# Chunk 1 of a two-product kernel in Strassen groups that accumulate on copies, with a new order of work

## The chip, the cores and the metric

The kernel runs on one core of a Trainium2 chip. The metric is device time in microseconds (us) of one execution; the median over several executions is compared. A core has a matrix engine (PE, with its weight loads PEld), three engines for element-wise work (DVE, which is VectorE; ACT, which is ScalarE; POOL, which is GpSimd) and SP (SyncE), which here only starts transfers. Matmuls write PSUM, a buffer of eight banks of 512 float32 per partition; SBUF is the other on-chip memory. Each engine takes its instructions in order and waits on semaphores for the others.

## The reference

Attention with linear cost comes first, then two matrix products with a SiLU between them. Shapes: q, k, v are (8 batches, 8 heads, 576 positions, 64), w_in is (512, 2048), w_out is (2048, 512), all float32.

```python
q_s = softmax(q over the 64 features)
k_s = softmax(k over the 576 positions)
kv  = k_s^T @ v                    # 64 x 64 for each batch and head
x   = q_s @ kv                     # regrouped as 4608 tokens x 512
h   = x @ w_in                     # 4608 x 2048
out = silu(h) @ w_out              # 4608 x 512
```

## The kernel before

**Stages.** Tokens are worked on in chunks of 512 (`TCH`), numbered 0 to 8. Chunk 0 is done as batch 0's whole 576 tokens, so chunk 1 holds only 448 new ones. For each batch `b` the kernel loads halves of q, k and v (`lq`, `lk`, `lv`, two halves each, 576 KB a half), takes exponentials on ACT (`eq`, `ek`), sums and normalises q (`z`, `n`), casts v (`vc`), transposes q (`tr` with copies `tc` for batches 0 and 1, a DMA transpose `tq` after them), multiplies k by v on PE (`kv`), normalises the result (`kc`), and multiplies q by it (`xt1` or `X`), which is copied out of PSUM as x (`x`, the suffix `a` or `v` says whether ACT or DVE does it).

**The first product** (x by w_in). Chunk 0 does 16 blocks `w0` to `w15` with 288-column matmuls, each followed by a tanh on ACT (`h`) and a multiply on DVE (`v`), which make the SiLU. Chunks 2 to 8 use a Strassen scheme (Winograd's form) with seven products in place of eight. The 2048 columns of w_in are split in two groups, g = 1 and g = 0; a group does products 1, 2, 6, 5, 7, 4, 3 of 8 matmuls each (`g{chunk}.{group}.{product}`), on operands that DVE has prepared (`WS` from w_in, `xs` from x). Products 1, 6, 7 and 4 accumulate in banks 0 and 1. After 1, 6 and 7 the running sum is copied to SBUF (`s`, line 400). Products 2, 5 and 3 go to another bank pair, and DVE adds each result to one of the copies (`a`, line 403). SiLU on ACT (`u`, line 409) reads three sums from SBUF and one from PSUM. Chunk 1 is half and half: group 1 so, with 224 columns, and group 0's eight blocks as plain products, `m0` to `m7`, four matmuls of 448 columns (line 335), with a SiLU each (`mu`, line 345).

**The second product** (by w_out). Chunk 0 does it plainly, `p0` to `p15`: block `p{i}` needs rows 128i to 128i+127 of w_out, and all four output tiles stand in banks 2 to 5 until `po` copies them out. Chunks 1 to 8 use Strassen products `b{chunk}.{product}.{half}` in banks 4 and 5 (line 503); `S` and `T` (line 487) are their operands, `sa`, `sb`, `sc`, `wa`, `wb`, `wc`, `wl` take the sums out, and `o` stores them. `e` are the products of the last chunk.

**Order.** One string, `ORDER`, lists every operation after a written-out start; the program calls them in that order, and each engine's queue is this list cut down to its own instructions. Nothing is reordered later. POOL starts all transfers of w_in (`load_w1`, line 564), w_out (`load_w2`: W2a, W2b1, W2b2, W2c1, W2c2, W2d, line 570) and of batches 1 and 2; SP starts the rest and the stores.

**Around the change.** W2b1 brings the rows for p4 and p5, W2b2 those for p6 and p7, W2c1 for p8 and p9, W2c2 for p10 and p11, W2d for p12 to p15. `kv1` needs v of batch 1, whose casts are `vc1.0` (whole, ACT), `vc1.1a` and `vc1.1b` (a half each on ACT and DVE). Buffers of loaded halves are two deep. `gcopy` and the `po` copies run on ACT and DVE between chunk 0's second product and chunk 1's first. The SiLU function and the exponential need different ACT tables; a change from one to the other is an `ACT_TABLE_LOAD`.

Of the kernel before, what the change touches and what calls it, by code (L numbers as in the profile page):

```python
# [8 lines left out]
FP32 = mybir.dt.float32  # L9
BF16 = mybir.dt.bfloat16  # L10
FP16 = mybir.dt.float16
ACT = mybir.ActivationFunctionType
# [6 lines left out]
    lk1.0 w1 lk1.1 w2 h1 w0 h2 v1 w3 h0 W2b1 w5 v0 v2 h3 w4 WS0.1 h5 w6 v3 h4 W2b2 v4 w7 v5 w8 h7 h6 v7 w9  # L19
    lv1.0 h8 v6 w11 v8 h9 lv1.1 w10 eq1.0.0 v9 h11 WS0.2 w12 eq1.1.0 v11 h10 w13 WS1.1 eq1.0.1 v10 h12 w15  # L20
    qp1a h13 v12 w14 eq1.1.1 v13 qp1b WS1.2 W2c1 p0 h14 z1.0 ek1.0 p1 z1.1.0 n1.0 z1.1.1 p2 h15 ek1.1 v15 p3
    WS1.4 W2c2 tr1.0 v14 lq2.0 p4 tc1.0a tc1.0b lq2.1 n1.1 p5 W2d p6 lk2.0 T1 vc1.0 lk2.1 p7 tr1.1 lv2.0
    vc1.1a vc1.1b gcopy WS1.3 kv1 lv2.1 tc1.1b p8 tc1.1a kc1 WS0.3 xt1.0 xt1.1 x1.0a x1.1v p9 x1.2a x1.3v
    g1.1.1 xs1.1 xs1.2 xs1.4 g1.1.2 s1.1.0a WS0.4 p10 xs1.3 eq2.0 a1.1.0 p11 eq2.1 z2.0 g1.1.6 g1.1.5
    s1.1.1a z2.1 n2.0 p12 ek2.0 g1.1.7 p13 s1.1.2v n2.1 ek2.1 p14 a1.1.2 g1.1.4 p15 tq2 u1.1.4 g1.1.3 po2v
    vc2.1 po1a m0 po3v po0a a1.1.1 u1.1.0 vc2.0 m1 lk3.0 mu0 m2 T2 lq3.0 mu1 lq3.1 m3 u1.1.2 lk3.1 T3 m4
    lv3.0 u1.1.1 lv3.1 m5 T4 mu2 os0 mu4 kv2 mu5 m6 mu3 kc2 X2.0 mu6 X2.1 x2.0v m7 x2.1a x2.3a x2.2v g2.1.1
    mu7 xs2.1 xs2.2 g2.1.2 s2.1.0v b1.1.0 ek3.0 S1.1 g2.1.6 eq3.1 lk4.0 S1.2 b1.2.0 os1 s2.1.1a b1.1.1 xs2.3
# [36 lines left out]
    qa10a e5.1 sc8 wcE0 e3.0 wcE1 qc01g wxE0 qc11a e3.1 wbE0 qc00a wxE1 qb00g qb01s e4.0 wbE1 qc10s qb10g
    e4.1 qb11s wlE0a ql01a ql00s wlE1a ql11a ql10s
# [4 lines left out]
def kernel(  # L71
# [206 lines left out]
    def xt_mm(b, cc, col, n, bank, dst):  # L278
        for r in range(2):
            for s in range(2):  # L280
                h = slice(s * 64, (s + 1) * 64)
                nc.tensor.matmul(  # L282
                    out=PS[r * 64:(r + 1) * 64, bank + s, dst:dst + n],
                    lhsT=kvn[b % 3][h, cc, r, :],
                    rhs=st[b]["qT"][h, col // P:(col + n) // P, cc, r * 64:(r + 1) * 64],
                )
# [44 lines left out]

    def mm1_mm(t, fb, bank, cs):
        o0 = pieces(t)[0][3]
        for c in cs:
            nc.tensor.matmul(  # L335
                out=PS[:, bank, o0:TCH],
                lhsT=W1[:, c, fb * 128:(fb + 1) * 128],
                rhs=XTS[t % 2][:, c, o0:TCH],
                start=(c == 0),
                stop=(c == NC - 1),  # L340
            )

    def mm1_out(t, fb, bank):
        o0 = pieces(t)[0][3]
        nc.scalar.activation(
            out=GTS[t % 2][:, fb, o0:TCH], in_=PS[:, bank, o0:TCH], func=ACT.Silu, scale=1.0 / XS
        )

    H = [None] * 3
# [38 lines left out]
    def four(t, i):  # L388
        return H[i].rearrange("p (f n) -> p f n", f=4)[:, :, 0:width(t)]

    def other(t, g):
        return 6 if t == 1 or g else 2

    def group_bank(t, g):
        bank = 0 if g is None else other(t, g)
        return PS[:, bank:bank + 2, :].rearrange("p b (f n) -> p (b f) n", f=2)[:, :, 0:width(t)]

    def group_snap(t, i, eng):
        H[i] = mp.tile([128, 2 * TCH], FP32, name=f"h{i}", bufs=1)
        copy(eng, four(t, i), group_bank(t, None))  # L400

    def group_add(t, g, i):
        nc.vector.tensor_tensor(  # L403
            out=four(t, i), in0=group_bank(t, g), in1=four(t, i), op=ALU.add
        )

    def group_silu(t, i, f, n):
        x = group_bank(t, None) if i is None else four(t, i)
        nc.scalar.activation(out=group_out(t, f, n), in_=x, func=ACT.Silu, scale=1.0 / XS)  # L409
# [429 lines left out]
```

## Time and profile before

| what | value |
|---|---|
| median of 3 executions | 257.08 us (256.99 to 257.14) |
| the profiled execution, whole | 258.61 us |
| the profiled execution, span of its instructions | 256.6 us |
| PE busy | 249.1 us, 97% |
| DVE, ACT, POOL busy | 206.2, 190.9, 65.8 us |
| groups' adds (line 403) | 45, mean 1206 ns |
| copies to SBUF on ACT (line 142, 1024 columns) | 29, mean 1010 ns |
| copies to SBUF on DVE (line 144, 1024 columns) | 13, mean 1222 ns |
| SiLU from SBUF / from PSUM (line 409, 1024 columns) | 1056 / 1020 ns |
| ACT table loads | 16, 1283 ns each |

A row of the timeline gives start (us from the span's start), length, engine, source line, operation, output and input with their shapes, and the count when several were merged; in square brackets is the engine's idle time before it and what ended that. Ends of matmuls are modelled, so the distance between starts is the safer measure. A row of the windows gives a stretch, its length, busy time and count of PE, PEld, DVE, ACT and POOL, the granted clock, the DMA engines' busy share (a 1 is all sixteen) and GB/s.

### The profile page before, as it was taken

What the parts mean: (1) busy time and instruction counts of PE and PEld (TensorE: products, weight loads), DVE (VectorE), ACT (ScalarE), POOL (GpSimd) and SP (SyncE); (2) the same over time, 40 slices, a digit from 0 to 9 for tenths busy, and PEclk for the clock granted to TensorE, in tenths of its full rate; (3) what the DMA queues carried; (4) which work ended last, traced back from release to release, by engine and by line L of the source; (5) the groups of instructions that cost most, each with busy time, mean ns of one, the idle gap of its engine ahead of it and who ended that gap; (6) DMA issues with size and microseconds to landing.
All of it is one profiled execution on the core that took longest, in us unless ns stands there. A gap on an engine that the chain in (4) does not pass through costs nothing.

```text
span 256.6 us, 6459 instructions
## 1 busy us (share of the span) xinstructions
PE 249.1 (97%) x2732; PEld 204.2 (80%) x2732; DVE 206.2 (80%) x276; ACT 190.9 (74%) x225; POOL 65.8 (26%) x62
## 2 busy tenths in 40 slices
PE   8799999999999999999999999999999999999994
PEld 3457746656888888888888888888888888888883
DVE  2958999888999898998987986896579836886752
ACT  5766876699999999999879988737587665664411
POOL 1753593650450622350073030006000000000022
PEclk9999999999999999999999999999999999999999
DMA  7999999979959957996874960021807000600365
GB/s 248 348 181 297 302 301 283 351 140 393 378 128 213 403 187 137 361 335 168 276 266 68 224 236 3 3 52 32 163 14 153 13 0 4 148 18 0 66 141 123
DMA packets 36044, 45.89 MB, mean 179 GB/s; under 512 B 16288, under 2 KB 21088, under 8 KB 36016
## 3 DMA queue, kind: packets, MB, share of 16 engines
q1 hardware_dynamic: 29456, 33.56, 45.5%
q0 software_dynamic: 6160, 11.60, 17.8%
q10 hardware_dynamic: 400, 0.33, 0.6%
q8 instruction: 21, 0.34, 0.5%
q14 instruction: 7, 0.06, 0.1%
HBM read 36.70 MB, written 9.44 MB: 180 GB/s over the span
## 4 chain that ended last, share of the span: by engine, by line
PE 76%; DMA 11%; issue 5%; POOL 3%; ACT 2%; DVE 1%; ACTq 0%; POOLq 0%
PE PS L503 37%; PE PS L425 33%; DMA qt<-in_q_dram 5%; DMA kt<-in_k_dram 5%; PE PS L335 3%; PE PS L248 2%; PE PS L282 2%; POOL W L564 1%; DMA out_dram<-ow 1%; POOL qt L152 1%; DVE GT L323 1%; ACT L409 0%; POOL W L570 0%; ACT sg L320 0%; ACT GT L409 0%
## 5 line engine op out<-in xcount | busy, mean ns | idle before, releaser
L403 DVE TENSOR_TENSOR h<-PS,h 128x1024 f32<-128x1024 f32 (+1 forms) x45 | 54.2, 1206 | 9.3 <-PE PS L425 7.8
L503 PEld LDWEIGHTS <-GT 128*128 128x128 f16 x512 | 50.1, 98 | 5.9
L425 PEld LDWEIGHTS <-WS 128*128 128x128 f16 x480 | 46.7, 98 | 6.5 <-issue 0.6
L409 ACT ACTIVATE GT<-h 128x1024 f16<-128x1024 f32 (+1 forms) x45 | 46.8, 1051 | 0.9 <-DVE h L403 0.7
L503 PE MATMUL PS<-W,GT 128*128 128x256 f16 x384 | 47.3, 273 | 0.0
L425 PE MATMUL PS<-XS,WS 128*128 128x256 f16 (+1 forms) x360 | 45.0, 272 | 0.0
L142 ACT COPY h<-PS 128x1024 f32<-128x1024 f32 (+1 forms) x31 | 31.1, 1003 | 16.9 <-PE PS L425 15.7
L503 PEld LDWEIGHTS <-S 128*128 128x128 f16 x384 | 37.1, 98 | 4.6
L425 PEld LDWEIGHTS <-W 128*128 128x128 f16 x360 | 35.2, 98 | 4.4
L216 POOL TENSOR_TENSOR eq<-eq,rzq 128x1152 bf16<-128x1152 bf16 x13 | 27.3, 2115 | 37.6 <-DVE rzq L211 36.3
L503 PE MATMUL PS<-T,S 128*128 128x256 f16 x256 | 32.2, 273 | 0.0
L144 POOL CAST vaug<-vt 128x1152 bf16<-128x1152 f32 x12 | 15.8, 1328 | 61.5 <-DMA vt<-in_v_dram 61.4
L425 PE MATMUL PS<-XT,W 128*128 128x256 f16 (+1 forms) x240 | 29.7, 272 | 0.0
L144 DVE COPY h<-PS 128x1024 f32<-128x1024 f32 (+1 forms) x14 | 17.0, 1212 | 9.2 <-PE PS L425 4.4
L207 DVE TENSOR_REDUCE zq<-eq 128x18 f32<-128x1152 bf16 x14 | 18.8, 1342 | 4.1 <-ACT eq L163 4.0
L163 ACT ACTIVATE eq<-qt 128x1152 bf16<-128x1152 f32 (+1 forms) x18 | 18.9, 1055 | 3.1 <-DMA qt<-in_q_dram 2.8
L168 ACT ACTIVATE ek<-kt 128x1152 bf16<-128x1152 f32 x16 | 18.6, 1163 | 3.0 <-DMA kt<-in_k_dram 2.9
L791 POOL DMA_DIRECT2D out_dram<-ow x5 | 2.7, 545 | 70.0 <-DVE ow L773 70.0
L409 ACT ACTIVATE GT<-PS 128x1024 f16<-128x1024 f32 (+1 forms) x15 | 15.2, 1013 | 6.1 <-PE PS L425 6.1
L503 PE MATMUL PS<-T,GT 128*128 128x256 f16 x128 | 16.3, 272 | 0.0
L307 PE MATMUL PS<-XT,W 128*128 128x288 f16 x128 | 16.0, 286 | 0.2 <-DMA W<-in_moe_w_in_dram 0.2
L503 PE MATMUL PS<-W,S 128*128 128x256 f16 x128 | 16.1, 273 | 0.0
(85 smaller groups left out, 332.4 us busy)
## 6 DMA issues: line engine op xcount, KB each, us to landing
out_dram<-ow SPq DMA_DIRECT2D x64, 128.0 KB, 3.0
qt<-in_q_dram SPq DMA_DIRECT2D x11, 576.0 KB, 5.9
kt<-in_k_dram SPq DMA_DIRECT2D x11, 576.0 KB, 7.5
vt<-in_v_dram SPq DMA_DIRECT2D x11, 576.0 KB, 6.6
qt<-in_q_dram POOLq DMA_DIRECT2D x4, 576.0 KB, 11.4
kt<-in_k_dram POOLq DMA_DIRECT2D x4, 576.0 KB, 13.9
vt<-in_v_dram POOLq DMA_DIRECT2D x4, 576.0 KB, 12.6
W<-in_moe_w_in_dram POOLq DMA_DIRECT2D x3, 512.0 KB, 10.6
```

Of the source, the lines that this page charges most:

```text
L142: eng.copy(out=o, in_=i)
L144: eng.tensor_copy(o, i)
L163: nc.scalar.activation(out=half(st[b]["eq"], cc)[:, :, g0:g1], in_=jgd(b, "qt", cc)[:, :, g0:g1], func=ACT.Exp)
L168: nc.scalar.activation(out=half(ek, cc), in_=jgd(b, "kt", cc), func=ACT.Exp)
L207: nc.vector.reduce_sum(out=z, in_=e, axis=AX.X)
L216: eng.tensor_tensor(out=e, in0=e, in1=r[:, :, :, None].to_broadcast([128, J, 2, D]), op=ALU.mult)
L307: nc.tensor.matmul(out=PS[:, WIDE[fb] + n, 0:S // 2], lhsT=W1[:, c, fb * 128:(fb + 1) * 128], rhs=XTS[0][:, c, n * (S // 2):(n + 1) * (S / ...
L335: nc.tensor.matmul(out=PS[:, bank, o0:TCH], lhsT=W1[:, c, fb * 128:(fb + 1) * 128], rhs=XTS[t % 2][:, c, o0:TCH], start=(c == 0), stop=(c ...
L403: nc.vector.tensor_tensor(out=four(t, i), in0=group_bank(t, g), in1=four(t, i), op=ALU.add)
L409: nc.scalar.activation(out=group_out(t, f, n), in_=x, func=ACT.Silu, scale=1.0 / XS)
L425: nc.tensor.matmul(out=PS[:, bank + p // 2, (p % 2) * HT:(p % 2) * HT + width(t)], lhsT=a[:, c, p * 128:(p + 1) * 128], rhs=bb[:, c, 0:wid ...
L503: nc.tensor.matmul(out=PS[:, bank, m * HN:(m + 1) * HN], lhsT=a[:, fc, m * 128:(m + 1) * 128], rhs=bb[:, fc, :], start=(first and fc == 0) ...
```

## The change

Chunk 1's group 0 becomes a Strassen group too; `m` and `mu` go. The scheme inside a group changes in all chunks. After product 1 the sum is copied from PSUM to a second bank pair (the seed, `s..1`), and product 2 accumulates there, on the copy. Product 5 goes to a third pair and is copied to SBUF (`s..5`). `a..12` adds the running sum after product 6 to that copy and writes the result back into the third pair in PSUM, where product 3 accumulates on it; `a..22` adds the sum after product 7 to the same copy, in SBUF. Product 4 accumulates on the running sum. SiLU now reads three sums from PSUM (`u..11`, `u..12`, `u..21`) and one from SBUF (`u..22`). The pairs of the two groups differ, so that group 0 can begin before group 1 has ended.

```diff
+    def pair_a(t, g):
+        return 2 if (t, g) == (1, 0) else 0
+    def pair_e(t, g):
+        return (4 if t == 1 else 6, 6 if t == 1 else 2)[g]
+    def pair_b(t, g):
+        return 6 if t == 1 else (2, 6)[g]
+    def seed(t, g, eng):
+        copy(eng, pair(t, pair_b(t, g)), pair(t, pair_a(t, g)))
+    def snap5(t, g, eng):
+        H5[g] = mp.tile([128, 2 * TCH], FP32, name=f"h{g}", bufs=1)
+        copy(eng, h5(t, g), pair(t, pair_e(t, g)))
+    def add12(t, g):
+        nc.vector.tensor_tensor(out=pair(t, pair_e(t, g)), in0=pair(t, pair_a(t, g)), in1=h5(t, g), op=ALU.add)
+    def add22(t, g):
+        nc.vector.tensor_tensor(out=h5(t, g), in0=pair(t, pair_a(t, g)), in1=h5(t, g), op=ALU.add)
...
     def group(t, g, i):
-        bank = 0 if i in (1, 6, 7, 4) else other(t, g)
+        bank = {2: pair_b(t, g), 5: pair_e(t, g), 3: pair_e(t, g)}.get(i, pair_a(t, g))
...
-                    start=(i in (1, 2, 5) and c == 0 and p % 2 == 0),
+                    start=(i in (1, 5) and c == 0 and p % 2 == 0),
...
-    for i in range(HF):
-        op(f"m{i}", mm1_mm, 1, FB[i], i % 4, range(NC))
-        op(f"mu{i}", mm1_out, 1, FB[i], i % 4)
...
     for fb in range(NFB):
-        op(f"w{fb}", wide_mm, fb, range(2 if fb in (0, 2) else 0, NC))
+        op(f"w{fb}.0", wide_mm, fb, (0, 1))
+        op(f"w{fb}.1", wide_mm, fb, (2, 3))
```

The written-out start becomes part of `ORDER`, in the same order on every engine up to w0. In x's product only the first matmul of a bank now carries the start flag. `kv2` uses banks 0 and 1 in place of 6 and 7. `ORDER` is new throughout, except that SP's instructions keep their order and the last chunk's second product keeps its own. The part for the end of chunk 0 and for chunk 1:

```
before: ... p0 ... tr1.0 ... p4 p5 p6 p7 tr1.1 kv1 p8 xt1.0 xt1.1 p9 g1.1.1 g1.1.2 p10 p11
        g1.1.6 g1.1.5 p12 g1.1.7 p13 p14 g1.1.4 p15 g1.1.3 m0 m1 m2 m3 m4 m5 kv2 m6 X2.0 X2.1 m7 g2.1.1
after:  ... p0 ... tr1.0 p4 p5 tr1.1 kv1 p6 xt1.0 xt1.1 p7 g1.1.1 p8 p9 g1.1.2 g1.1.6 p10 p11
        g1.1.5 p12 p13 p14 p15 g1.1.3 g1.1.7 g1.0.1 g1.0.5 g1.1.4 g1.0.6 g1.0.2 kv2 g1.0.7 X2.1 X2.0
        g1.0.3 g1.0.4 g2.1.1
POOL's transfers after W2a
before: lk1.0 lk1.1 W2b1 W2b2 lv1.0 lv1.1 W2c1 W2c2 lq2.0 lq2.1 W2d lk2.0 lk2.1 lv2.0 lv2.1
after:  lk1.1 lv1.1 lk1.0 W2b1 lv1.0 W2b2 W2c1 lq2.0 lq2.1 lk2.0 W2c2 W2d lk2.1 lv2.1 lv2.0
```

(PE's operations alone in the first four lines.)

More of the change, by code (lines that the diff above doesn't have):

```diff
@@ L18 @@
 ORDER = """
[L19 to L28, printed above, removed]
@@ new lines @@
+    kc0.1 heat3 x0.0a x0.0v X0.1 w0.0 x0.1a w2.0 x0.1v w1.0 w0.1 w1.1 h0 w3.0 h1 w3.1 w2.1 v0 w4.0 v1 h2 w4.1 h3
+    w5.0 v2 w5.1 lk1.1 h4 v3 h5 w6.0 WS0.1 v4 w6.1 lv1.1 w7.0 h6 w7.1 w8.0 w8.1 WS1.1 v5 h7 v7 w9.0 w9.1 h8 v6 lk1.0
+    w11.0 h9 eq1.0.0 v8 v9 w10.0 W2b1 w11.1 WS0.2 w10.1 eq1.0.1 w12.0 lv1.0 h11 w13.0 w12.1 qp1a v11 W2b2 w13.1
+    eq1.1.0 z1.1.0 w15.0 h10 w15.1 h12 W2c1 h13 v10 qp1b w14.0 w14.1 v12 eq1.1.1 v13 p0 lq2.0 z1.0 h15 p1 ek1.1 p2
+    h14 z1.1.1 p3 v15 WS1.3 n1.0 ek1.0 tr1.0 vc1.1a n1.1 tc1.0a vc1.0 vc1.1b p4 v14 WS1.2 p5 tc1.0b tr1.1 tc1.1b kv1
@@ new lines @@
+    p6 gcopy kc1 lq2.1 WS0.3 tc1.1a xt1.0 x1.0a lk2.0 x1.1v xt1.1 x1.2a p7 g1.1.1 W2c2 eq2.0 p8 x1.3v eq2.1 T1 p9
+    s1.1.1v xs1.1 g1.1.2 xs1.2 g1.1.6 z2.1 W2d lk2.1 xs1.4 u1.1.11 z2.0 p10 xs1.3 ek2.0 lv2.1 p11 g1.1.5 s1.1.5a p12
+    p13 ek2.1 lv2.0 p14 p15 po1a WS1.4 a1.1.12 T3 po0a n2.1 po2v po3v g1.1.3 g1.1.7 g1.0.1 WS0.4 u1.1.12 n2.0 vc2.1
+    g1.0.5 a1.1.22 s1.0.1v g1.1.4 u1.1.22 T2 vc2.0 tq2 s1.0.5a lk3.0 lq3.0 g1.0.6 g1.0.2 u1.1.21 lq3.1 kv2 a1.0.12
+    u1.0.11 kc2 g1.0.7 X2.1 lk3.1 X2.0 a1.0.22 x2.3a g1.0.3 x2.0v x2.1a u1.0.12 x2.2v xs2.1 u1.0.22 g1.0.4 lv3.0
@@ L276, in pieces, with xt_mm @@
         return got
-    def xt_mm(b, cc, col, n, bank, dst):
+    def xt_mm(b, cc, col, n, bank, dst, start=True):
         for r in range(2):
@@ L330, in wide_out @@
         )
[L332 to L349, printed above, removed]
     def span(t, n):
@@ L386, in group_out @@
         return GTS[t % 2][:, f:f + 4, span(t, n)]
[L388 to L409, printed above, removed]
     def group(t, g, i):
-        bank = 0 if i in (1, 6, 7, 4) else other(t, g)
+        bank = {2: pair_b(t, g), 5: pair_e(t, g), 3: pair_e(t, g)}.get(i, pair_a(t, g))
+        o0, w0 = pieces(t)[0][3], width(t)
         w, f0, f1 = WS[g], 4 * g + 8, 4 * g
@@ L432, in group, with pair, h5, silu4 @@
                 )
+    H5 = [None] * 2
+    def pair_a(t, g):
[4 more added lines that the diff above has]
+        return 6 if t == 1 else (2, 6)[g]
+    def pair(t, bank):
+        return PS[:, bank:bank + 2, pieces(t)[0][3]:TCH]
+    def h5(t, g):
+        return H5[g].rearrange("p (b n) -> p b n", b=2)[:, :, pieces(t)[0][3]:TCH]
+    def seed(t, g, eng):
[7 more added lines that the diff above has]
+        nc.vector.tensor_tensor(out=h5(t, g), in0=pair(t, pair_a(t, g)), in1=h5(t, g), op=ALU.add)
+    def silu4(t, g, x, f, n):
+        x = h5(t, g) if x is None else pair(t, x)
+        o = group_out(t, f, n)
+        nc.scalar.activation(
+            out=o.rearrange("p (b f) n -> p b f n", b=2),
+            in_=x.rearrange("p b (f n) -> p b f n", f=2), func=ACT.Silu, scale=1.0 / XS
+        )
     def rows(t, col):
@@ L689 @@
         if b > 1:
-            bank = 2 if b in KV_WITH_X.values() else 6
+            bank = 2 if b in KV_WITH_X.values() else 0 if b == 2 else 6
             op(f"tq{b}", q_transpose, b)
@@ L717 @@
                 op(f"g{n}{i}", group, t, g, i)
-            for i, f, h in ((0, 4 * g + 8, 0), (1, 4 * g + 8, 1), (2, 4 * g, 1)):
-                both(f"s{n}{i}", group_snap, t, i)
-                op(f"a{n}{i}", group_add, t, g, i)
-                op(f"u{n}{i}", group_silu, t, i, f, h)
-            op(f"u{n}4", group_silu, t, None, 4 * g, 0)
+            both(f"s{n}1", seed, t, g)
+            both(f"s{n}5", snap5, t, g)
+            op(f"a{n}12", add12, t, g)
+            op(f"a{n}22", add22, t, g)
+            for x, bank, f, h in (
+                ("11", pair_b(t, g), 4 * g + 8, 0),
+                ("12", pair_e(t, g), 4 * g + 8, 1),
+                ("21", pair_a(t, g), 4 * g, 0),
+                ("22", None, 4 * g, 1),
+            ):
+                op(f"u{n}{x}", silu4, t, g, bank, f, h)
     for t in range(1, last):
```

164 lines of the change are left out of this document (69 added, 95 removed).

## The prediction

> **What bounds the kernel now.** I read the page's busy shares first, then the windows by stage, the PE timeline of chunk 1, the chain, and last the rows that price an operation.
>
> ```profile
> PE 249.1 (97%) x2732; PEld 204.2 (80%) x2732; DVE 206.2 (80%) x276; ACT 190.9 (74%) x225; POOL 65.8 (26%) x62
> ...
> DMA  7999999979959957996874960021807000600365
> ```
>
> PE is busy nearly throughout, so a gain must come out of PE's own stream or out of its few gaps. The DMA engines are full from the second slice (6.4 us) to about 51 us. The stages, in the windows (us of the window, then busy us of PE, PEld, DVE, ACT, POOL, clock, DMA share):
>
> ```profile
> 31.00:45.00 14.00, 13.89 (x162) 7.61 (x160) 13.76 (x27) 9.95 (x13) 8.79 (x11) 1.00 1.13 289
> 45.00:62.00 17.00, 16.10 (x183) 9.97 (x182) 14.77 (x18) 14.46 (x22) 7.44 (x4) 1.00 0.89 282
> 62.00:87.00 25.00, 25.00 (x338) 22.01 (x337) 23.96 (x31) 24.53 (x26) 9.81 (x7) 1.00 0.89 275
> 112.00:253.00 141.00, 140.94 (x1523) 124.79 (x1508) 108.93 (x138) 96.08 (x110) 16.86 (x14) 1.00 0.41 102
> ```
>
> From 62 us on PE has no room to give. Only the stage that the change rewrites, 31 to 62 us, has gaps, and two of PE's rows there carry a releaser; a DMA ends the one and ACT the other:
>
> ```profile
> 45.62 1.70 PE L425 MATMUL PS<-XS,WS 128*128 128x224 f16 x16
> 47.62 1.02 PE L445 MATMUL PS<-W,GT 128*128 128x512 f16 x4 [0.30 <-DMA W<-in_moe_w_out_dram]
> 48.48 0.93 PE L425 MATMUL PS<-XS,WS 128*128 128x224 f16 x8
> ...
> 52.60 0.93 PE L425 MATMUL PS<-XT,WS 128*128 128x224 f16 x8
> 54.13 4.70 PE L335 MATMUL PS<-XT,W 128*128 128x448 f16 x24 [0.60 <-ACT GT L409]
> ```
>
> Starts are exact, ends are modelled, so I count start to start: eight 224-column matmuls take 0.77 us (48.48 to 49.25), four 448-column ones 0.76 (24 from 54.13 to 58.76, less the small break before kv2), four 512-column ones 0.86, eight 256-column ones 0.87. The group from 45.62 took 2.00 for 1.53 of work, so p12 (the product with the last quarter of W2) lost 0.46; m0 started 1.53 after g1.1.3 instead of 0.77, so it lost 0.76. The ACT rows show that m0's wait is a DMA's too:
>
> ```profile
> 36.56 1.16 ACT L142 CAST vaug<-vt 128x1152 bf16<-128x1152 f32 x1 [0.63 <-DMA vt<-in_v_dram]
> 38.02 0.67 ACT L142 CAST vaug<-vt 128x576 bf16<-128x576 f32 x1 [0.30 <-DMA vt<-in_v_dram]
> ...
> 49.17 1.16 ACT L168 ACTIVATE ek<-kt 128x1152 bf16<-128x1152 f32 x1 [1.52 <-DMA kt<-in_k_dram]
> 50.69 1.16 ACT L168 ACTIVATE ek<-kt 128x1152 bf16<-128x1152 f32 x1 [0.35 <-DMA kt<-in_k_dram]
> 51.87 1.28 ACT L409 ACT_TABLE_LOAD   x1
> 53.16 0.92 ACT L409 ACTIVATE GT<-PS 128x896 f16<-128x896 f32 x1
> ```
>
> The chain that ended last goes the same way, through the transfer of lk2.1, ACT's table load and SiLU, to m0:
>
> ```profile
> 38.30 12.31 DMA kt<-in_k_dram
> ...
> 51.87 1.28 ACT L409
> ...
> 54.13 4.70 PE PS L335 x24
> ```
>
> Two equal loads become usable 1.46 to 1.52 us apart: the POOL queue's transfers land one after another in issue order. Their completion events in the trace (last part of each) give W2a 29.6, lk1.0 31.1, lk1.1 32.6, W2b1 33.7, W2b2 35.0, lv1.0 36.5, lv1.1 38.0, W2c1 39.1, W2c2 40.4, lq2.0 41.9, lq2.1 45.7, W2d 47.6, then k and v at 1.5 steps. A q, k or v half costs 1.5, a 256 KB piece of W2 1.1 to 1.3. At lq2.1 one part came about 2 us late, and W2d kept that lateness.
>
> **The change, part by part.**
>
> *PE work.* It removes m0 to m7, 8 x 0.757 = 6.05, and adds seven products of 0.767, 5.37: -0.69. All of it is on PE, hence on the path. All other matmuls are the same in number and shape.
>
> *DVE and ACT work.* Fourteen groups lose a copy and an add each: DVE loses 14 x 1.214 of adds and seven copies of 1.22, ACT seven of 1.01. Chunk 1 gains an add and a copy on DVE (2.2), and four SiLU of about 0.95 for eight L345 rows of 0.57. So DVE is some 23 us and ACT some 7 us less busy. I cost this at nothing: from 62 us on PE covers both engines.
>
> *Copies and adds that write PSUM.* No row has VectorE or ScalarE writing PSUM. The nearest are 1.214 (add from PSUM) and 1.01 or 1.22 (copies out of PSUM); I take these.
>
> ```profile
> 231.82 1.91 PE L425 MATMUL PS<-XS,WS 128*128 128x256 f16 x16
> 232.96 1.22 DVE L144 COPY h<-PS 128x1024 f32<-128x1024 f32 x1 [1.17 <-PE PS L425]
> ```
>
> The first eight of these matmuls end at 231.82 + 0.87 = 232.69; the copy starts 0.27 later. With 0.1 for the way back an add needs 1.58 and an ACT copy 1.36, in the two PE slots (1.75) that the new order mostly leaves between a product and the next one on the same banks. Shorter writes are worth nothing, since PE covers them. As the upper bound I take the worst stretch of any DVE row, T3's, which ran beside POOL's casts:
>
> ```profile
> 56.36 2.17 DVE L487 TENSOR_TENSOR W<-W 128x2048 f16<-128x2048 f16 x1
> 58.45 1.21 DVE L487 TENSOR_TENSOR T<-W,T 128x2048 f16<-128x2048 f16 x1
> ```
>
> By that ratio, 1.8, an add would be 2.17 long and its product 0.8 late. [...]
>
> *Start.* All engines have the same order up to w0. In w0 to w3 the first halves now stand together, so of w1's 0.37 wait on the second W1 piece about 0.1 is left. p0 starts near 30.9 instead of 31.02, and the gain is lost at p4, below.
>
> *POOL's transfers.* New order after W2a: lk1.1, lv1.1, lk1.0, W2b1, lv1.0, W2b2, W2c1, lq2.0, lq2.1, lk2.0, W2c2, W2d. By the steps above W2b1 lands at 35.2, lv1.0 36.7, W2b2 37.8, W2c1 39.1, lk2.0 43.6, W2c2 44.7, W2d 47.0; if a part is again 2 us late at 43, W2c2 lands at 46.6 and W2d at 48.9. SyncE's queue is as before, and what it waits for (n2.1 on POOL, near 50) is not later.
>
> *PE's walk through chunk 1.* p0 30.9, p3 ends 34.35, tr1.0 34.87 (n1.0 is now ready, so 0.28 goes). p4 waits for W2b1 until 35.25, as early as before. After tr1.1 (37.5) kv1 waits for lv1.0 plus the whole 1.16 cast, which had been the halved one: 38.0. It ends at 38.7; p6, xt1.0 at 39.7 (kc1, 0.97 behind kv1 as in the trace), p7 to 41.0, g1.1.1, p8, p9, g1.1.2 at 43.6, g1.1.6 to 45.15. p10 then waits for W2c2, 1.4 if it is late; p11, g1.1.5, p12 at 49.1, p15 ends 52.6. Before, p15 also ended at 52.60, but with two more groups done.
>
> *The end of chunk 1.* From 52.6: g1.1.3, g1.1.7, g1.0.1, g1.0.5 to 55.67. On DVE, T3 (1.21 to 2.17 beside POOL's casts), two output copies and WS0.4 stand ahead of add a1.1.22, which so ends at 56.1: g1.1.4 waits 0.5. The seed of g1.0 follows on DVE, and before it ACT must load its table again (1.28; there are 18 loads, 16 before) and free the bank pair by u1.1.12: g1.0.6 waits 0.3. g1.0.2, kv2 (behind u1.1.21, 0.1), g1.0.7, X2 (behind kc2 and u1.0.11, 0.15), g1.0.3, g1.0.4: end 62.66. Before, g2.1.1 starts at 61.69. So chunk 2 begins +0.97 late.
>
> *Chunks 2 to 8.* Same PE work. Before loses 0.25 in three hand-offs (66, 95, 105 us), which I let go. In chunk 2 kv3 must wait for u2.1.11 to empty banks 6 and 7, at the end of an ACT queue of two table loads: 11.6 us after g2.1.1 against 11.35, +0.25. The tail from e1.0 has the same order.
>
> *Sum.* +0.97 - 0.25 + 0.25 = +0.97. The profiled execution took 258.61 (span 256.6); on its basis 259.6. It stands 1.5 above the median of 257.08, so the forecast is 258.05, say 258.0.
>
> **Rivals.** 0.2% (0.5 us) is about what a measurement of this kernel tells from no change.
>
> *No late part (faster).* The late part stood in one execution, and may not stand in the timed ones. W2c2 at 44.7 and W2d at 47.0 are then in time; p15 ends at 51.1, g1.1.4 and g1.0.6 wait 0.9 together, and g2.1.1 comes at 61.1, -0.56: 256.5. Without the waits on DVE, 255.6. It decides by W2d landing before 47.6. Against it: a before without the late part also gains, up to 1.2, since m0 hangs on lk2.1. Chance 0.25.
>
> *A draw.* Late part, but T3 at 1.21 and no table wait: +0.1 to +0.5, 257.4. Chance 0.2.
>
> *Later chunks wait.* ACT's or DVE's queue is late at one add in each of seven chunks, 0.2 each: 259.4. For it: slack of only 0.17 in 1.75; against it: before had such slots throughout and lost 0.25. Chance 0.1.
>
> *PSUM writes are slow.* 0.8 for each of 16 first adds: 270. Nothing in the trace speaks for it. Chance 0.03.
>
> *Change not done as said.* The new order does have the products and copies that it names; no chance.
>
> **How the numbers follow.** The forecast case has 0.42. Its own range is 257.5 to 258.8 (waits on DVE 0.4 to 1.5). The range for 8 in 10 reaches over the draw and part of the faster case, and up to late chunks: 256.3 to 259.3. Faster by over 0.2%: 0.25. Same: 0.2, the draw. Slower: 0.42 + 0.1 + 0.03 = 0.55.
>
> **What would show it.** Right: kv1 near 38.0 released by ACT's cast; p10 or p12 released by a DMA of w_out; g1.1.4 released by DVE; g2.1.1 at 62 or later; no PE gap over 0.3 after 65. Wrong: p15 ending by 51.5, g2.1.1 before 61.2, or adds (L403's heirs) over 1.4 us, which would put gaps at every group.

## The result

The changed kernel is slower: 261.52 us, median of 4 executions (261.43 to 262.32), against 257.11 (256.99 to 257.73, 4 executions) of the kernel before on the same chip. The ratio is 1.0173, 95% interval 1.0147 to 1.0199. The prediction was 258.0 with a range to 259.3, so it had the side right and missed the size by 3.5 us; the time lies 2.2 us above the end of the range. The profiled execution took 261.43, its span is 259.6.

First its page, PE's line and the DMA engines' line, then the same four windows as before (us of the window, then busy us of PE, PEld, DVE, ACT, POOL, clock, DMA share, GB/s).

```profile
PE 250.0 (96%) x2756; PEld 206.6 (80%) x2756; DVE 189.2 (73%) x257; ACT 186.0 (72%) x216; POOL 68.1 (26%) x62
...
DMA  7999999799549955998690991004803030070265
```

```profile
31.00:45.00 14.00, 13.71 (x163) 8.14 (x162) 13.24 (x23) 11.17 (x14) 7.31 (x9) 1.00 1.14 303
45.00:62.00 17.00, 15.58 (x202) 11.61 (x201) 16.39 (x22) 13.63 (x16) 7.81 (x4) 1.00 0.94 304
62.00:87.00 25.00, 22.76 (x272) 19.90 (x270) 23.00 (x26) 23.29 (x25) 9.31 (x6) 1.00 0.75 224
112.00:253.00 141.00, 141.00 (x1534) 124.48 (x1533) 92.16 (x122) 92.54 (x107) 18.53 (x13) 1.00 0.42 105
```

The third window is the finding. From 62 to 87 us PE was busy for all 25.00 us before; now it is busy for 22.76, though DVE, ACT and the DMA engines all do less there. PE's rows in the timeline name who ends its waits, two in chunk 1 and two in chunk 2:

```profile
51.68 0.93 PE L386 MATMUL PS<-XT,WS 128*128 128x224 f16 x8 [0.65 <-DVE PS L421]
...
55.60 0.93 PE L386 MATMUL PS<-XS,W 128*128 128x224 f16 x8 [0.69 <-DVE h L424]
```

```profile
70.34 1.03 PE L386 MATMUL PS<-XS,WS 128*128 128x256 f16 x8 [1.21 <-DVE PS L421]
...
78.56 1.03 PE L386 MATMUL PS<-XS,WS 128*128 128x256 f16 x8 [1.02 <-DVE kvn L260]
```

Start to start these cost 0.81 (ahead of g1.1.3), 0.86 (g1.1.4), 1.38 (g2.1.7) and 1.19 us (g2.0.5), 4.24 in all. No DMA ends any of them, and between p0 and e1.0 PE has no other wait over 0.34. All four wait for DVE, but the add that releases g2.1.7 has its normal length; what is long stands ahead of it in DVE's queue:

```profile
48.01 2.60 DVE L356 TENSOR_TENSOR WS<-W,WS 128x1024 f16<-128x1024 f16 x1
50.54 1.08 DVE L421 TENSOR_TENSOR PS<-PS,h 128x896 f32<-128x896 f32 x1
...
65.84 1.21 DVE L476 TENSOR_TENSOR S<-GT 128x2048 f16<-128x2048 f16 x1
67.09 2.06 DVE L476 TENSOR_TENSOR S<-S,GT 128x2048 f16<-128x2048 f16 x1
69.07 1.22 DVE L421 TENSOR_TENSOR PS<-PS,h 128x1024 f32<-128x1024 f32 x1
...
75.00 2.88 DVE L486 TENSOR_TENSOR T<-W,T 128x2048 f16<-128x2048 f16 x1
...
78.02 0.49 DVE L260 TENSOR_TENSOR kvn<-PS,rz 128x128 bf16<-128x128 f32 x2
```

WS1.4 (48.01) takes 0.68 elsewhere, S1.2 (67.09) and T4 (75.00) 1.21 to 1.22. What all three have beside them is a row of POOL:

```profile
45.73 4.34 POOL L215 TENSOR_TENSOR eq<-eq,rzq 128x1152 bf16<-128x1152 bf16 x2 [5.47 <-DVE rzq L210]
...
66.11 1.97 POOL L143 CAST vaug<-vt 128x1152 bf16<-128x1152 f32 x1 [0.45 <-DMA vt<-in_v_dram]
...
74.69 2.12 POOL L215 TENSOR_TENSOR eq<-eq,rzq 128x1152 bf16<-128x1152 bf16 x1 [0.52 <-DVE rzq L210]
```

T4 ends at 77.88, 1.07 after POOL's multiplication (76.81); S1.2 at 69.15, 1.07 after the cast (68.08); WS1.4 at 50.61, 0.54 after n2 (50.07). Each therefore stood still until POOL's instruction had ended and then ran its own length less 0.14 to 0.15. It goes the other way too: the cast of 66.11 takes 1.16 alone, and ended 1.03 after S1.1 (67.05), which had started first. The chain that ended last shows the same for S1.2: of its time, 1.62 us are "issue", in which DVE waited for nothing that the profile shows:

```profile
65.92 1.14 DVE S L476
67.06 0.02 issue
67.09 0.36 DVE S L476
67.44 1.62 issue
69.07 1.22 DVE PS L421
```

Not every DVE operation is hit. The one-input reduction z (line 206) has 1.34 beside POOL as elsewhere; the add of 50.54, whose operand in PSUM is one of two, has 1.08 beside a cast. Over the whole run float16 DVE operations with both inputs in SBUF are stretched by 7.5 us in all, against 2.2 in the profile of before, where T3's row of 2.17 (shown in the prediction) was one of them, and no matmul waited behind them. (These sums take each shape's usual length as its own.)

This was the theory for the experiments: **a lock between DVE and POOL**. The new order puts such DVE operations where POOL works and ahead of adds that PE waits for. Rivals: POOL's work as a whole is a burden (traffic, its queue), whichever instruction stands beside it; or the new order is late by itself and the stretches are only seen beside it.

### The profile page after: what moved, and what is told of

The parts are those of the page before. It is cut to its first block, busy times and chain, and to the rows that moved or that the text cites. A ratio compares the mean times of both kernels' runs of the same rounds, so it can differ in the third digit from the quotient of the medians.

```text
span 259.6 us, 6498 instructions
## 1 busy us (share of the span) xinstructions
PE 250.0 (96%) x2756; PEld 206.6 (80%) x2756; DVE 189.2 (73%) x257; ACT 186.0 (72%) x216; POOL 68.1 (26%) x62
## 4 chain that ended last, share of the span: by engine, by line
PE 65%; DVE 8%; issue 2%; DMA 1%; ACT 1%; ACTq 0%; DVEq 0%
PE PS L502 32%; PE PS L386 30%; DVE zq L206 1%; PE PS L281 1%; DVE XS L366 1%; PE PS L247 1%; DVE S L476 1%; DVE PS L421 1%; DVE h L424 1%; DVE PS L143 1%; DMA out_dram<-ow 1%; DVE ow L522 0%; DVE kvn L260 0%; DVE rzq L210 0%; DVE ow L748 0%
## 5 line engine op out<-in xcount | busy, mean ns | idle before, releaser
L429 ACT ACTIVATE GT<-PS 128x1024 f16<-128x1024 f32 (+1 forms) x48 | 47.1, 1010 | 19.7 <-PE PS L386 17.8
L386 PEld LDWEIGHTS <-WS 128*128 128x128 f16 x512 | 49.8, 98 | 9.5 <-issue 3.9
L386 PE MATMUL PS<-XS,WS 128*128 128x256 f16 (+1 forms) x384 | 48.7, 271 | 2.3 <-DVE PS L421 1.2
L386 PE MATMUL PS<-XT,W 128*128 128x256 f16 (+1 forms) x256 | 32.7, 271 | 0.0
L421 DVE TENSOR_TENSOR PS<-PS,h 128x1024 f32<-128x1024 f32 (+1 forms) x16 | 19.4, 1213 | 15.6 <-PE PS L386 11.7
L424 DVE TENSOR_TENSOR h<-PS,h 128x1024 f32<-128x1024 f32 (+1 forms) x16 | 19.2, 1198 | 7.0 <-PE PS L386 7.0
L143 DVE CAST XT<-PS 128x512 f16<-128x512 f32 (+1 forms) x17 | 11.1, 678 | 12.6 <-PE PS L281 12.6
L167 ACT ACTIVATE ek<-kt 128x1152 bf16<-128x1152 f32 x16 | 18.5, 1162 | 1.9 <-DMA kt<-in_k_dram 1.9
L429 ACT ACTIVATE GT<-h 128x1024 f16<-128x1024 f32 (+1 forms) x16 | 16.7, 1045 | 1.6 <-DVE h L424 1.6
L386 PE MATMUL PS<-XS,W 128*128 128x256 f16 (+1 forms) x128 | 16.4, 271 | 0.8 <-DVE h L424 0.7
L386 PE MATMUL PS<-XT,WS 128*128 128x256 f16 (+1 forms) x128 | 16.4, 271 | 0.6 <-DVE PS L421 0.6
```

The lines of the kernel that those rows point to most:

```text
L143: eng.tensor_copy(o, i)
L167: nc.scalar.activation(out=half(ek, cc), in_=jgd(b, "kt", cc), func=ACT.Exp)
L386: nc.tensor.matmul(out=PS[:, bank + p // 2, o0 + (p % 2) * w0:o0 + (p % 2 + 1) * w0], lhsT=a[:, c, p * 128:(p + 1) * 128], rhs=bb[:, c, 0:w0],
L421: nc.vector.tensor_tensor(out=pair(t, pair_e(t, g)), in0=pair(t, pair_a(t, g)), in1=h5(t, g), op=ALU.add)
L424: nc.vector.tensor_tensor(out=h5(t, g), in0=pair(t, pair_a(t, g)), in1=h5(t, g), op=ALU.add)
L429: nc.scalar.activation(out=o.rearrange("p (b f) n -> p b f n", b=2), in_=x.rearrange("p b (f n) -> p b f n", f=2), func=ACT.Silu, scale=1. ...
```

## The experiments

**The kernel before, once more.** No edit.

> The kernel before, unchanged, profiled once more. Its first profile took 258.61 against a median of 257.1, and had one part of the lq2.1 transfer 2 us late. If that late part is what the timed executions lack: W2d lands near 45.7 to 46.5, p12 starts without a wait, m0 starts near 53.0 instead of 54.13, span near 255.2. If the difference lies elsewhere: the same waits of 0.46 and 0.76 in chunk 1.

It took 257.36, span 255.3. Here the late part of the prediction's profile is absent: m0 waits 0.28 instead of 0.76, g2.1.1 starts at 60.40 instead of 61.69 and the tail's first product, e1.0, at 238.39 instead of 239.68. From 62 to 87 us PE is busy for all 25.00 here too. So the first profile of before was 1.3 us longer than most of its executions, and profile to profile the change costs 259.6 - 255.3 = 4.3 us: 1.58 up to g2.1.1 (61.98), 2.75 from there to e1.0 (242.72).

**POOL's normalisations and casts of blocks 2 to 7 left out,** in both kernels:

```
-    ... n2.1 po2v po3v g1.1.3 ... n2.0 vc2.1
+    ... po2v po3v g1.1.3 ...                    (n2 to n7 and vc2 to vc7 dropped likewise)
```

> The changed kernel without POOL's element-wise work of batches 2 to 7: the normalisation of q (n2 to n7) and the cast of v (vc2 to vc7) are left out, so q goes on unnormalised and v of batch 1 is used throughout. Port theory (a DVE subtraction or addition with two float16 inputs in SBUF stands still while POOL works, and the new order puts seven of them beside POOL, just ahead of adds that PE waits for): no stretched DVE row after 40 us, the waits of 0.81, 0.86, 1.38, 1.19 and 0.37 on PE go, 261.5 - 4.4 = 257.1 (256.4 to 257.8). Rival (the new scheme's hand-offs through PSUM are too long for the slots): the waits stay, 260.5 or more.

> The kernel before with the same POOL work left out. Port theory: its few stretched DVE rows are ahead of no add that PE waits for, so 257.1 - 0.3 = 256.8 (256.3 to 257.2); and the changed kernel without POOL work is then within 0.7 of it. Rival: this gains as much as the changed kernel does (3 to 4), POOL being a general burden.

The changed kernel fell to 257.97 (span 255.6), ratio to before 1.0025 (1.0003 to 1.0046). The kernel before stayed at 258.03 (span 255.7), 1.0013 (0.9998 to 1.0027). Both times lie above the ranges expected for them (256.4 to 257.8 and 256.3 to 257.2), by 0.2 and 0.8 us. The waits ahead of g1.1.3, g2.1.7 and g2.0.5 are gone, g1.1.4's is 0.34. DVE's rows, to be set beside 48.01 and 50.54 above:

```profile
47.45 0.68 DVE L356 TENSOR_TENSOR WS<-W,WS 128x1024 f16<-128x1024 f16 x1
49.13 1.10 DVE L421 TENSOR_TENSOR PS<-PS,h 128x896 f32<-128x896 f32 x1 [1.01 <-ACT h L141]
```

So POOL's work costs the one kernel 3.6 us by the medians, 4.0 by the spans, and the other none. A general burden would have paid in both; it falls. Leaving the work out also takes away every wait for its results, so this pair alone does not single out the lock; the moves and the pieces below do. And the rest of the change, without POOL's work, is worth nothing that can be measured (spans of 255.6 and 255.7).

**Block 2's normalisation alone left out** (n2.0 and n2.1):

> The kernel after without POOL's normalisation of block 2 alone (n2.0 and n2.1, two of the twelve; block 2's heads go on unnormalised). Lock theory, now by the single instruction: the subtraction WS1.4 and the product sum xs1.3 that stood beside n2.0 and n2.1 take 0.68 and 0.33 us, the matmuls of g1.1.3 do not wait (0.81 before), those of g1.1.4 wait 0.3 to 0.4 instead of 0.86, and chunk 2's first group starts 1.3 us earlier (60.7 instead of 61.98); the waits of chunk 2 before g2.1.7 (1.38) and g2.0.5 (1.19), which stand beside vc3 and n3, stay: 260.2 us, between 259.7 and 260.7. Rival (it is POOL's sum of work): a sixth of the 4 us, 260.9, and no wait gone whole.

It took 260.98 (260.12 to 261.85), 0.3 outside the expected range, and the time is nearer to the rival's 260.9 than to the lock's 260.2. Only the rows speak for the lock, and by them it is half a hit: g1.1.3's wait is gone and g2.0.5's stays at 1.18. But the casts of v, which wait for their transfers, fell otherwise: one now stood beside WS0.4 (1.54 instead of 0.68), and g1.1.4 waited 1.18 instead of 0.3 to 0.4. In chunk 2 the cast met S1.1 (2.17) instead of S1.2, and g2.1.7 waited 0.52. So the hits went from WS1.4 and S1.2 to WS0.4 and S1.1 with no DVE instruction moved.

**The victims moved in the order,** POOL's work untouched:

```
-    ... po1a WS1.4 a1.1.12 ...            S1.2 a2.1.12 z3.0 g2.1.7 a2.1.22 ...   b1.5.0 T4 n3.1 ... S1.3 b1.5.1
+    ... xs1.2 WS1.4 ... po1a a1.1.12 ...  a2.1.12 S1.2 g2.1.7 a2.1.22 z3.0 ...   b1.5.0 n3.1 ... S1.3 T4 b1.5.1
```

> The changed kernel complete, with four DVE operations moved in the order: WS1.4 ahead of z2.1, S1.2 behind a2.1.12, z3.0 behind a2.1.22, T4 behind S1.3. Port theory: a1.1.12, a2.1.12 and kc3 start on time, PE's waits before g1.1.3, g2.1.7 and g2.0.5 (0.81, 1.38, 1.19) go, the one before g1.1.4 shrinks by some 0.1 to 0.8: 258.1 (257.6 to 258.6). Rival of slow hand-offs: 260.5 or more, the waits stay at these three places.

A miss: 262.54 (262.16 to 262.85; ratio 1.0200, 1.0169 to 1.0232), no faster than the changed kernel. The three named waits went, as they should if they belong to these instructions; g1.1.4's fell to 0.07. But now S1.4 was issued beside n3:

```profile
74.86 2.83 DVE L476 TENSOR_TENSOR S<-GT,S 128x2048 f16<-128x2048 f16 x1
```

```profile
82.50 1.03 PE L386 MATMUL PS<-XS,WS 128*128 128x256 f16 x8 [0.98 <-DVE PS L421]
...
85.89 0.27 PE L502 MATMUL PS<-T,GT 128*128 128x256 f16 x1 [1.48 <-ACT sc L518]
```

The DVE instructions behind S1.4 came late and g2.0.7 waited 1.14; then b1.4.1 waited 1.64 for the snapshot sc1, a wait that the next runs explain. Before that, b1.5.0 waited 0.98 for DVE's wa1, behind the two reductions z3, and in chunk 1 p10 waited 0.54 for W2c2.

**POOL's instructions cut in pieces,** three or nine, in the changed kernel, and three in the kernel before:

```
-        eng.tensor_tensor(out=e, in0=e, in1=r[..].to_broadcast([128, J, 2, D]), op=ALU.mult)
+        n = 3 if eng is nc.gpsimd and b > 1 else 1            (9 in the second; vcast likewise)
+        for i in range(n):
+            j = slice(i * J // n, (i + 1) * J // n)
+            eng.tensor_tensor(out=e[:, j], in0=e[:, j], in1=r[:, j, ..].to_broadcast([128, J // n, 2, D]), op=ALU.mult)
```

> The kernel after, with each of POOL's normalisations (n2 to n7) and casts of v (vc2 to vc7) cut in three pieces of 3 of the 9 columns j; same places, same work, 48 more instructions on POOL. Lock theory (a float16 VectorE operation with two inputs in SBUF stands still until the running POOL instruction has ended): an instruction of POOL now lasts about 0.71 us (n) or 0.5 (vc) instead of 2.13 and 1.46, so no stretch is over about 0.7: the last subtraction of weights, WS1.4, takes at most 1.4 instead of 2.60, S1.2 1.9 instead of 2.06 to 1.3, T4 1.9 instead of 2.88. The waits before g1.1.3 (0.81), g1.1.4 (0.86), g2.1.7 (1.38) and g2.0.5 (1.19) fall to about 0.1, 0.6, 0.6 and 0.3 or less: 258.6 to 259.6 us, 259.0. Rival (VectorE stands still until POOL has no work left, or what stretches it is the traffic itself): POOL's stretches of work are as long as before or longer, the waits stay, 261.5.

> As the split in three, but in nine pieces of one column each: an instruction of POOL lasts about 0.24 us if its time goes by its size, and has a fixed part on top that no run has shown. Lock theory: stretches of at most 0.3 us, waits as with POOL's work left out (1.3 us of waits in that run), 258.0 us; if the fixed part is large, POOL's n and vc end later, tq2, tq3 and kv3 with them, and PE waits there instead: up to 259.5. Rival (the traffic or all of POOL's queue counts): 261.5 or more.

> The kernel before with the same cut in three. Lock theory: its VectorE operations are stretched by 2.2 us in all, but no matmul waits for one of them, so nothing is to be had: 257.1 to 257.5. Rival (smaller POOL instructions are good for something else, or bad by their fixed part): what this kernel moves by is taken off the result of the kernel after; over 0.5 either way would say that.

Measured 263.62 (262.01 to 264.79), 269.17 (268.39 to 269.81) and, for before, 257.81 (256.85 to 259.73; ratio 1.0021, 0.9999 to 1.0043). Before lies 0.3 above its range but cannot be told from no change; the two others miss by far.

In three pieces the lock theory is right row by row: WS1.4 took 1.31, S1.2 1.23, T4 1.59, and the waits ahead of g1.1.3, g2.1.7 and g2.0.5 are gone, g1.1.4's is 0.70; kv3 starts at 72.60 instead of 74.88. But the gain runs into the next limit:

```profile
69.80 6.86 POOL L221 TENSOR_TENSOR eq<-eq,rzq 128x384 bf16<-128x384 bf16 x6
```

```profile
83.14 1.16 ACT L162 ACTIVATE eq<-qt 128x1152 bf16<-128x1152 f32 x1 [3.75 <-DMA qT<-eq]
```

```profile
85.89 3.57 PE L506 MATMUL PS<-T,GT 128*128 128x256 f16 x16 [3.60 <-ACT sc L522]
```

n3's six pieces took 6.86 us, not 6 x 0.71: a piece is 0.83 long alone, and the last two were 1.81 each, held up by T4 and S1.4, which had got the lock between two pieces. n3.1 ended at 76.66, the transpose tq3 was issued at 76.69 (76.84 in the changed kernel), and fifteen of its sixteen parts had landed by 81.50, the last at 83.04. In the changed kernel the last landed at 81.48. So about 1.5 us of the wait are one late part, and why it was late no run here shows. ACT's eq4.0 needs the buffer that tq3 reads; sc1 is queued behind eq4.0 and ek4.1, and b1.4.1 waits for sc1. In the changed kernel PE came to this place 3.4 us later (85.54 against 82.13), and there was no wait. The wait also cost more than its length. The windows (clock third from the end):

```profile
85.00:86.50 1.50, 0.61 (x4) 0.41 (x4) 0.63 (x2) 1.48 (x3) 1.43 (x5) 0.50 1.06 404
86.50:88.00 1.50, 1.50 (x9) 1.04 (x8) 1.40 (x3) 1.49 (x2) 0.91 (x2) 0.50 1.03 368
88.00:89.50 1.50, 1.50 (x9) 1.03 (x8) 0.20 (x2) 1.09 (x2) 1.17 (x2) 0.50 1.02 396
89.50:91.00 1.50, 1.50 (x9) 1.04 (x8) 0.69 (x1) 0.00 (x0) 1.23 (x2) 0.50 1.04 411
91.00:93.00 2.00, 2.00 (x17) 1.63 (x15) 0.00 (x0) 1.80 (x2) 0.00 (x0) 0.83 1.05 406
```

After the 3.6 us without a matmul the granted clock was 0.50, by the last window until about 91.7 (an estimate: 0.83 as a mean of 0.50 and 1.00): products of 0.87 took up to 1.71, 2.8 us lost on top of the 3.76. The four executions had mean clocks from 1.000 (262.01 us) to 0.986 (264.79 us), so not all of them paid this in full.

In nine pieces WS1.4 got in between two pieces (0.88), but for T4 the lock did not open:

```profile
74.52 6.48 POOL L221 TENSOR_TENSOR eq<-eq,rzq 128x128 bf16<-128x128 bf16 x18
```

```profile
76.46 5.62 DVE L490 TENSOR_TENSOR T<-W,T 128x2048 f16<-128x2048 f16 x1
```

The 18 pieces follow each other at 0.36 us (0.24 would be a ninth of 2.12; the other 0.12 came with each piece), and T4, issued at 76.46, stood through all that were left, until 81.00, and ended 1.08 later. g2.0.5 waited 3.60 for kc3 behind it, again followed by a clock of 0.50 (83.96 to 87.38); kv2 and kv5, which wait for the last casts, took 2.61 and 2.38 instead of 0.74 and 0.62. So short pieces helped here only where DVE's instruction got in between two of them (WS1.4, 0.88, against T4, 5.62); what decides that, these runs do not show.

**POOL's work given to DVE and ACT:**

```
-                op(f"n{b}.{c}", qnorm, b, c, nc.gpsimd)
+                op(f"n{b}.{c}", qnorm, b, c, nc.vector)
...
-                op(f"vc{b}.{c}", vcast, b, c, nc.gpsimd)
+                op(f"vc{b}.{c}", vcast, b, c, nc.scalar)
```

> The kernel after with POOL's n2 to n7 given to VectorE (1.35 us each by the row of n0 and n1.1, 12 of them, 16.2 us) and vc2 to vc7 to ScalarE (1.16 each by its row, 14 us), at the same places in the order. No POOL instruction is left to block anything, so the stretches go, as in the run that left this work out (255.6 us of span); the price is what the two engines' queues pay: in chunk 1 (n2.0, n2.1 on a VectorE that had 1.4 us idle from 50 to 58) and in chunk 2 the adds come up to 1.3 later each. Lock theory: below the kernel after if these delays cost less than the 4 us that the stretches do; estimate 259.5, between 258 and 261.5. Rival (POOL's work costs nothing, the order itself is late): 261.5 plus the added work, 262.5 or more.

Far off: 277.77 (277.37 to 278.13). After 34 us no stretch is left there, but the queues pay some 20 us (277.8 against the 258.0 of the run without POOL's work), where I had allowed 2: g1.1.4 waits 2.70, b1.4.1 4.05 (with a clock of 0.50 behind it, 91 to 96 us), and there are waits of 0.6 to 1.6 in chunks 3 to 5. DVE and ACT, each busy for 72% of this run, have room on average and none where the adds and snapshots are due.

**Three pieces, and DVE kept away from n3:**

```
-    ... b1.5.0 T4 n3.1 g2.0.1 kc3 ... g2.0.5 S1.4 tq3 S1.3 b1.5.1 ... ek4.1 a2.0.12 sc1
+    ... b1.5.0 n3.1 g2.0.1 kc3 ... g2.0.5 tq3 S1.3 T4 b1.5.1 ... ek4.1 a2.0.12 S1.4 sc1
```

> The kernel after with POOL's work in three pieces, as before, and two VectorE instructions moved: T4 from ahead of kc3 to behind S1.3, S1.4 from ahead of S1.3 to behind the add a2.0.12. In the run with three pieces the four waits had gone but a new one had come, 3.76 us ahead of the product b1.4.1 (then 0.78, 0.83, 0.83 and 0.36 behind it): ScalarE stood from 79.4 to 83.14 ahead of eq4.0, until the transpose tq3 had landed, and the snapshot sc1 was queued behind it; tq3 waits for n3.1, whose last two pieces took 1.81 us each instead of 0.83 beside T4 and S1.4. Theory: the lock works both ways, POOL's pieces stand still while a two-input VectorE operation runs; with T4 and S1.4 out of the way n3.1 ends at about 74.9 instead of 76.66, tq3 lands 1.8 earlier, and the 6.6 us of waits fall to 2 or less: 258.3 us, between 257.3 and 260. Rival (the wait is not tq3's, or tq3's landing is set by traffic and not by its issue): 262 or more.

It took 260.18 (260.0 to 260.62), 3.4 less than without the move and just above the expected range. POOL's six pieces were 0.83 each, n3.1 ended at 75.20, tq3 was issued at 75.22 instead of 76.69. What is left of the 6.6 us is one wait of 1.78 ahead of b1.4.1, with the clock at 1.00 throughout, because tq3's last part landed at 81.55. The issue came 1.47 earlier and the landing 1.49, so the theory holds for both. What keeps the landing at 6.3 us after the issue, where the changed kernel has 4.6, is again one part of sixteen: the other fifteen had landed by 79.94.

**An attempt at a faster kernel, and a second with one transfer moved:**

```
(casts of v in three pieces, n left whole; T4 and S1.4 as above, and)
-    xs1.2 g1.1.6 z2.1 ...  po1a WS1.4 a1.1.12 ...  WS0.4 u1.1.12 ... a1.1.22 s1.0.1v g1.1.4
+    xs1.2 g1.1.6 WS1.4 z2.1 ...  po1a a1.1.12 ...  u1.1.12 ... a1.1.22 s1.0.1v WS0.4 g1.1.4
(second:)
-    kc1 lq2.1 ... lk2.0 ... g1.1.1 W2c2
+    kc1 W2c2 lq2.1 ... lk2.0 ... g1.1.1
```

> An attempt at a kernel faster than both: the change kept, POOL's casts of v cut in three (n left whole), WS1.4 moved ahead of z2.1 (a time at which POOL does nothing), WS0.4 from ahead of the add a1.1.22 to behind the seed s1.0.1, T4 behind S1.3 and S1.4 behind a2.0.12. Lock theory: of the waits of the kernel after, those before g1.1.3 (0.81), g1.1.4 (0.86), g2.1.7 (1.38) and g2.0.5 (1.19) go to 0.3 or less in all, those of 0.1 to 0.26 stay (2 us in all): a span of 255.4, 257.1 us, between 256.4 and 258.5. If the change were worth its 0.7 us of matmuls, the lower half of this; if the lock only moves to other instructions once more, 259 to 262.

> The attempt before, with one more move: on POOL's queue the transfer W2c2 goes ahead of lq2.1 instead of behind lk2.0 (the kernel before has it ahead of both lq2 transfers). There W2c2 landed at 45.78 us and p10 waited 0.33 for it, W2d at 48.34 and p12 waited 0.07, where one of lk2.0's 16 parts came about 1.1 late; now W2c2 has two transfers less ahead of it and lands near 42.5 to 43.5, and lq2.1 and lk2.0 about 1 us later, which eq2.1 and ek2.0 pay on ScalarE. Expectation: the waits of p10 and its like go, 258.3 us, between 257.6 and 258.9; it stays 0.2 to 0.5% behind the kernel before, since what is left (g1.0.6 0.43, some 0.1 each elsewhere) is spread. Rival (the late part is paid in any order, now by eq2.1 and z2.1): 258.8 or more.

258.82 (258.21 to 259.88; ratio 1.0062, 1.0042 to 1.0082) and 258.65 (258.06 to 260.08; 1.0046, 1.0019 to 1.0074). In the first all four waits named are gone (0.3 us in all had been allowed), tq3 landed at 79.69, with no late part, and eq4.0 did not wait. The time still missed its range by 0.3. PE's waits (total, times, longest) are now mostly of another kind:

```profile
PE PS L556 <- DVE XS L548: 1.2, 1, 1.2
PE PS L447 <- DMA W<-in_moe_w_out_dram: 0.7, 2, 0.5
PE PS L250 <- ACT vaug L141: 0.6, 2, 0.3
PE PS L389 <- DVE PS L143: 0.3, 1, 0.3
PE PS L389 <- DVE PS L424: 0.3, 1, 0.3
```

The first of these stands in the opening of every kernel here, before chunk 0; only the last is a wait for an add. The second attempt is inside its range. It removed the wait for W2c2, and the timed runs can't tell it from the first: its profiled execution began chunk 1 late by 1.1 us, after a wait of 0.88 for a piece of W1. About two thirds of the loss can be had back by keeping DVE's two-input operations and POOL apart; no version here beats the kernel before.

## Why the prediction was right and wrong

**PE work, -0.69: right.** The groups of 224 columns take 0.77 each in both kernels. With POOL's work left out of both, chunk 2 begins at 60.56 against 60.32: the 0.69 is used up by new waits, the largest 0.34, 0.34 and 0.24 ahead of tr1.1, g1.1.4 and g1.0.6.

**DVE and ACT work "at nothing: from 62 us on PE covers both engines": the step that failed.** DVE is less busy, 189.2 against 206.2 us: 17.0 less where 23 had been counted, and the stretches (7.5 against 2.2) are most of the difference. The cover broke all the same, since PE waits for single adds that stand behind single stretched operations. 2.57 of the 2.75 us lost from chunk 2 on are the two waits ahead of g2.1.7 and g2.0.5. The waits behind WS1.4 in chunk 1, g1.1.3's 0.81 and 0.52 of g1.1.4's 0.86, make 1.33 more. Together 3.9 of the 4.3.

**Copies and adds that write PSUM: value right, bound put to the wrong use.** The adds into PSUM measure 1231 ns against 1214 for those into SBUF, 17 more, and ACT's copies into PSUM 1010 as before. The way back, put at 0.1, is 0.06 where an add releases g1.1.3 (51.62 to 51.68) and 0.05 where kc3 releases g2.0.5 (78.51 to 78.56). The rival of slow writes is out. The bound came from T3's row of 2.17 "beside POOL's casts". I read it as a ratio, 1.8, that might befall any add. By the rows of these runs it is a standstill until POOL's instruction ends (T4 ended 1.07 after it), it befalls DVE operations with two inputs in SBUF, and adds out of PSUM are spared (1.08 beside a cast). The row was on the table; what I did not ask is which such operations the new order issues while POOL runs, and who is queued behind them.

The lock itself rests on these rows: T4 took 2.88 instead of 1.21 beside POOL's multiplication, the cast 1.97 instead of 1.16 beside S1.1, and T4 stood 4.5 us through a train of short pieces. By what means the two engines hold each other up, no run here shows.

**Start, POOL's transfers, the walk: right, but for the late part.** p0 started at 30.85 (30.9 forecast), W2b1, lv1.0, W2c2 and W2d landed at 35.03, 36.52, 44.59 and 47.15 (35.2, 36.7, 44.7, 47.0), kv1 at 37.76 (38.0). No part came late, so p12 started at 47.41 instead of 49.1 and p15 ended near 50.9, which the prediction had named as a sign against its forecast. That was the condition of the faster rival. It did not make the kernel faster, because of the four waits, and because a before without the late part gains as well, as the prediction had said against it.

**The basis.** The profile of before held 1.3 us of late part that most executions do not have. Taking off 1.5 was the right amount; but the sum of +0.97 had been made with the late part on both sides. Without it the same steps give g2.1.1 at 61.1, 0.7 after before's 60.40, so the base did not cause the miss.

**The end of chunk 1.** g1.1.4 waited 0.86 (0.5 forecast, by the right instructions: T3, two copies, WS0.4), g1.0.6 0.24 (0.3). g1.1.3's 0.81 was not foreseen. That chunk 2 began at 61.98, near the forecast's 62.66, is luck: the late part was missing, and the waits behind WS1.4 stood in its place.

**Chunks 2 to 8, sum 0; rival "later chunks wait", 0.2 in each of seven.** The rival named the right engine and the wrong pattern: chunk 2 alone lost 2.6 us and the later ones next to nothing, the window from 112 to 253 being full. POOL is busy for 9.31 of the 25 us after 62 and for 18.5 of the 141 after 112, where DVE also has 49 us idle. The sign "no PE gap over 0.3 after 65" failed twice, with the 1.38 and the 1.19. kv3 waited 0.09, as in the kernel before, where 0.25 had been added for it.

What stays open is the last 0.5% between the last attempts and the kernel before. Waits for transfers in the opening that differ from execution to execution (p0 between 30.55 and 32.15 in these profiles) may make up part of it; no run here separates them.

## What to carry to other kernels

When an order is rewritten, list for each POOL instruction the DVE operations with two SBUF inputs that will be issued beside it, and look at what is queued behind them: a stretched row in the old profile (here T3's 2.17) is a warning for the new one even where nobody waited for it. Moving one victim can hand the place to the next, as WS1.4, S1.2 and T4 did to S1.4, so a gain has to be followed to the next limit, here a transpose, a buffer and a snapshot behind them on ACT. Take two profiles of the base before subtracting one of its waits.

## What the runs showed of the hardware

- **The lock worked both ways, and a train of pieces could starve DVE.** T4 was held 1.67 us by one POOL instruction, and 4.5 us through a train of 0.36 us pieces; POOL's pieces of 0.83 took 1.81 beside T4 and S1.4. Not every train did so: WS1.4 took 0.88 beside such pieces. One-input operations (z, 1.34) and adds with an operand in PSUM (1.08) kept their length beside POOL.
- **A piece of POOL's multiplication took 0.12 us more** than its share of the whole one's 2.12: a ninth went at 0.36 instead of 0.24, a third took 0.83 instead of 0.71.
- **Three long waits of PE were followed by half clock.** After 3.6 and 3.9 us without a matmul (three pieces; POOL's work on DVE and ACT) the granted clock was 0.50 for 6.8 us, after 3.4 us (nine pieces) for 3.4 us; after 1.6 us (three pieces, DVE kept away from n3) and 2.3 us (POOL's work on DVE and ACT) it stayed at 1.00. Such a gap is not the only case: with nine pieces the clock was also 0.50 from 60.07 to 63.48, where PE had no gap over 0.64 but kv2's small matmuls, which wait for POOL's casts, took 2.61 us instead of 0.74.
- **One part of sixteen was late in some runs.** Fifteen of tq3's sixteen parts landed 4.6 to 4.8 us after the issue in the changed kernel, in the run with the victims moved and in both runs with n in three pieces; in all of these but the changed kernel the sixteenth came 1.5 to 1.6 us after them.
